# Four large scalings of an output pass, each with its store, cut in two halves

## The chip, the cores and the metric

The kernel runs on one core of one Trainium2 chip. The metric is the device time of one execution in microseconds (us), as the median of several runs. A profiled execution of the same program supplies the trace.

## The reference

The input `x` has 384 x 384 positions of 384 channels, in bfloat16 (one batch). The kernel scales every channel by a gate worked out from that channel's mean over all positions:

```python
g = jnp.einsum("bhwc->bc", x) / (H * W)
s = jax.nn.sigmoid(g * w1d[0])        # k = 1
return x * s[:, None, None, :]
```

So the whole input has to be summed before the first output can be written: 113 MB are read, the gate is found, and 113 MB are written. The on-chip memory does not hold the whole input.

## The kernel before, in words

**Rows.** The 147456 positions are spread over 128 partitions, 1152 rows of 384 channels to each partition. A "row" below is one such row on all 128 partitions, 96 KB. The chip's memory holds an `arena` of 275 rows. A load or a store of n rows is one DMA of 128 pieces of n x 768 bytes. The chunk `STREAMED` (784 rows and one more) passes through the arena and is read a second time later; the chunk `KEPT` stays on the chip between the passes.

**Pass one** loads all rows and sums them on TensorE into the PSUM tile `acc`. Part of the kept rows is packed meanwhile: in a group, the fourth row of every four is hidden in unused bits of the other three (`fold`), so that three rows of memory hold four. There are ten groups (`GROUPS`), of 16, 24 or 32 rows; the last is kept in PSUM banks (`BANKED`). Then ScalarE works out the gate (`s_bf`, with a copy `s_ps` in PSUM).

**Pass two** follows an order that is written out by hand, `PLAN2`. Its entries, with arena addresses:
- `("M", a, n, m)`: scale n rows from address a. DVE (VectorE) does the first n - m rows and POOL (GpSimd) the last m; POOL's part first waits for the DVE instruction that stands before DVE's part (`scale_both`).
- `("W", a, n)`: store n rows from address a (`store`).
- `("L", a, n)`: load the next n streamed rows to address a (`load`).
- `("U", g, a, m)`: the next of five steps that unpack group g: `fields`, `signs` and `three` are bit operations on DVE (lines 280 and 286), `threefold` and `fourth` scale its rows.
- `("B", a)`: bring the PSUM group back to the arena (ScalarE).

Scaling is line 444, storing line 465, loading line 240.

**Order and waits.** Every engine goes through its own entries in the order written. All loads and stores are issued by SP (SyncE) on one queue, in the order of the `W` and `L` entries. The class `Flow` keeps for every row who wrote it and who read it, and puts a semaphore wait in front of an instruction for each such dependence: a store waits for the scalings of its own rows, a load waits for the stores that still read the rows it overwrites. An SP instruction that waits holds up all SP instructions behind it. The semaphores of SP's DMAs go round in 24 lanes, and a DMA also waits for the one 24 before it.

Of the kernel before, what the change touches and what calls it, by code (L numbers as in the profile page):

```python
# [131 lines left out]
def kernel(  # L132
# [13 lines left out]
    B, H, W, C = x.shape  # L146
# [14 lines left out]
    U = 3 * PIECE + PAIRS * 3 * PAIR  # L161
# [424 lines left out]
    for a, n in ((U, 4), (U + 4, 4), (V, 4)):  # L586
# [102 lines left out]
```

## Time and profile before

| | |
|---|---|
| median of 3 runs | 722.63 us (722.34 to 723.5) |
| profiled execution | 719.44 us, of which the trace's span is 717.3 us |
| data moved | 303.70 MB, mean 423 GB/s over the span |
| busy time: DVE, POOL, ACT, PE | 468.8, 119.1, 116.5, 223.3 us |
| chain that ended last | DMA 44%, DVE 29%, PE 16% of the span |

The trace's times count from its first instruction. Pass one ends at about 268 us; pass two takes the rest. In the page's slices each digit is the busy share of one fortieth of the span, in tenths. The chain of work follows back from the last instruction, at each step to what released it. For a DMA the trace has the time of its issue on SP and the time from issue to landing (all its bytes at their place).

### The profile page before, as it was taken

Reading aid. Unit: us, or ns where it says so; the run is one execution under the profiler, and the core shown is the slowest. Engines: PE = TensorE matmul, PEld = TensorE weight load, DVE = VectorE, ACT = ScalarE, POOL = GpSimd, SP = SyncE. Lnnn points to the kernel's source line nnn. Section 1 sums busy time; section 2 is a strip of 40 time slices with the busy share of each in tenths; the row PEclk is TensorE's granted clock in tenths of the full one; section 3 lists DMA queues with packets and bytes.
Section 4 is the critical chain, followed back from the end, with each engine's and each line's share of the span. In section 5 each row is a group of like instructions: output and inputs, shape, how many; then the busy total and the mean of one; then the engine's idle time right before and its main releaser. Section 6 shows DMA issues by size and latency. Waiting matters only on the chain.

```text
span 717.3 us, 2076 instructions
## 1 busy us (share of the span) xinstructions
PE 223.3 (31%) x1279; PEld 0.3 (0%) x3; DVE 468.8 (65%) x359; ACT 116.5 (16%) x97; POOL 119.1 (17%) x43
## 2 busy tenths in 40 slices
PE   4577977999998880000000000000000000000000
PEld 0000000000000000000000000000000000000000
DVE  4600001798989849997999999979189950366800
ACT  3700001576767630000000020000000000000000
POOL 0000000000000006608024143562114400000000
PEclk9889988999999995555555555555555555555555
DMA  9999999999999989999999999999999999999997
GB/s 378 429 445 422 434 441 437 430 433 426 427 426 428 431 334 386 399 428 432 432 430 438 432 434 433 450 413 451 415 456 426 434 437 401 455 439 396 450 426 323
DMA packets 15853, 303.70 MB, mean 423 GB/s; under 512 B 1762, under 2 KB 2402, under 8 KB 5474
## 3 DMA queue, kind: packets, MB, share of 16 engines
q1 hardware_dynamic: 15840, 303.57, 98.9%
q8 instruction: 5, 0.08, 0.0%
q14 instruction: 6, 0.05, 0.0%
q10 hardware_dynamic: 2, 0.00, 0.0%
HBM read 190.32 MB, written 113.25 MB: 423 GB/s over the span
## 4 chain that ended last, share of the span: by engine, by line
DMA 44%; DVE 29%; PE 16%; POOL 2%; DVEq 1%; ACT 1%; issue 1%; SPq 0%; POOLq 0%
DMA arena<-in_x_dram 33%; DVE arena L444 17%; PE bank L246 16%; DMA out_dram<-arena 11%; DVE arena L280 7%; DVE arena L286 5%; POOL arena L444 2%; DVEq L107 1%; ACT arena L317 1%; SPq L240 0%; ACT s_bf L431 0%; SPq L465 0%; SPq L113 0%; POOLq L113 0%; SPq L684 0%
## 5 line engine op out<-in xcount | busy, mean ns | idle before, releaser
L280 DVE TENSOR_SCALAR arena<-arena 128x1536 uint16<-128x1536 uint16 (+2 forms) x199 | 149.4, 795 | 128.3 <-DMA arena<-in_x_dram 98.5
L246 PE MATMUL bank<-arena,ones 128*128 128x384 bf16 x1151 | 202.8, 339 | 35.4 <-DMA arena<-in_x_dram 35.3
L444 POOL TENSOR_TENSOR arena<-arena,s_bf 128x1536 bf16<-128x1536 bf16 (+7 forms) x39 | 118.9, 3062 | 444.7 <-ACT bank L435 268.2
L444 DVE TENSOR_TENSOR arena<-arena,bank 128x1152 bf16<-128x1152 bf16 (+21 forms) x57 | 159.9, 2846 | 7.4 <-DMA arena<-in_x_dram 7.0
L317 ACT ACTIVATE arena<-arena 128x3072 uint16<-128x3072 uint16 (+1 forms) x38 | 102.5, 2696 | 146.0 <-DVE arena L280 146.0
L286 DVE TENSOR_TENSOR arena<-arena 128x3072 uint16<-128x3072 uint16 (+2 forms) x90 | 117.6, 1307 | 13.0 <-PE bank L246 10.1
L541 PE MATMUL bank<-odd,ones 128*128 128x1 bf16 x1 | 0.2, 187 | 316.2 <-DVE odd L536 316.2
L444 DVE TENSOR_TENSOR arena<-arena,s_bf 128x11136 bf16<-128x11136 bf16 (+4 forms) x7 | 46.6, 6699 | 59.0 <-DMA arena<-in_x_dram 48.6
L382 ACT COPY arena<-bank 128x512 uint32<-128x512 uint32 (+2 forms) x8 | 4.2, 534 | 155.3 <-DMA out_dram<-arena 155.1
L246 PE MATMUL bank<-s_bf,ones 128*128 128x384 bf16 x125 | 22.1, 326 | 0.0
L317 ACT ACTIVATION_READ_ACCUMULATOR arena<-arena 128x1 f32 x38 | 7.1, 187 | 0.0
L382 ACT COPY bank<-arena 128x512 uint32<-128x512 uint32 (+2 forms) x8 | 3.8, 527 | 0.0
L260 PE MATMUL bank<-arena,ones 128*128 128x384 bf16 x1 | 0.5, 478 | 6.6 <-DMA arena<-in_x_dram 6.6
L431 ACT ACTIVATE s_bf<-bank,w_sc 128x384 bf16<-128x384 f32 x1 | 0.6, 581 | 9.7 <-PE bank L246 9.7
L657 ACT ACT_TABLE_LOAD x1 | 1.3, 1283 | 0.7 <-PEq L673 0.7
L347 DVE TENSOR_SCALAR w_sc<-bank 128x1 f32<-128x1 f32 x1 | 0.2, 160 | 1.3 <-PE bank L342 1.3
L342 PE MATMUL bank<-w_bf,ones 1*128 1x1 bf16 x1 | 0.2, 182 | 2.5 <-DMA w_bf<-in_w1d_dram 2.5
L337 DVE MEMSET ones<- 128x128 bf16 x1 | 0.2, 165 | 1.0 <-PEq L673 1.0
L541 PEld LDWEIGHTS bank<-odd,ones 128*128 128x128 bf16 x1 | 0.1, 105 | 574.4 <-DVE odd L536 574.4
L545 DVE CAST odd_i<-bank 128x1 int32<-128x1 f32 x1 | 0.2, 157 | 0.3 <-PE bank L541 0.3
L435 ACT COPY bank<-s_bf 128x192 uint32<-128x192 uint32 x1 | 0.3, 323 | 0.0
L382 ACT COPY arena<-rest 128x64 uint32<-128x64 uint32 x1 | 0.2, 245 | 0.0
(10 smaller groups left out, 1.4 us busy)
## 6 DMA issues: line engine op xcount, KB each, us to landing
arena<-in_x_dram SPq DMA_DIRECT2D x4, 8160.0 KB, 39.5
out_dram<-arena SPq DMA_DIRECT2D x4, 8160.0 KB, 26.7
out_dram<-arena SPq DMA_DIRECT2D x7, 3072.0 KB, 23.7
arena<-in_x_dram SPq DMA_DIRECT2D x6, 3072.0 KB, 19.4
arena<-in_x_dram SPq DMA_DIRECT2D x3, 4608.0 KB, 24.5
arena<-in_x_dram SPq DMA_DIRECT2D x2, 4992.0 KB, 23.3
arena<-in_x_dram SPq DMA_DIRECT2D x2, 4512.0 KB, 36.9
out_dram<-arena SPq DMA_DIRECT2D x2, 4512.0 KB, 26.2
```

The costliest lines, as they stand in the source:

```text
L107: with self.tc.tile_critical(sync_engine=mybir.EngineType.Pool, no_gpsimd_drain=True):
L246: return pe.add_instruction(mybir.InstMatmult(name=nc.get_next_instruction_name(), ins=[pe.lower_ap(rhs), pe.lower_ap(ones[:])], outs=[pe. ...
L260: return nc.tensor.matmul(acc, lhsT=ones[:], rhs=arena[:, i, :], start=first, stop=last)
L280: lambda: nc.vector.tensor_scalar(out=dst, in0=src, scalar1=s0, scalar2=s1, op0=op0, op1=op1),
L286: "DVE", lambda: nc.vector.tensor_tensor(out=dst, in0=a, in1=b, op=op), reads=reads, writes=writes
L317: lambda: nc.scalar.activation(out=y, in_=y, func=ACTF.Copy, accum_out=seen[:, 2 * k + i : 2 * k + i + 1]),
L382: "ACT", lambda: nc.scalar.copy(dst.bitcast(u32), src.bitcast(u32)), reads=reads, writes=writes
L431: lambda: nc.scalar.activation(out=s_bf[:], in_=acc, func=ACTF.Sigmoid, scale=w_sc[:, 0:1]),
L435: "ACT", lambda: nc.scalar.copy(s_ps.bitcast(u32), s_bf[:].bitcast(u32)), reads=["s_bf"], writes=["bank0"]
L444: lambda: vec.tensor_tensor(out=v, in0=v, in1=s[:, None, :].to_broadcast([P, n, C]), op=Op.mult),
L541: lambda: nc.tensor.matmul(votes, lhsT=ones[:], rhs=odd[:], start=True, stop=True),
L657: nc.scalar.preload_act_table(ACTF.Sigmoid)
```

## The change

Four `M` entries of `PLAN2` become two each, and so do the `W` entries that store their rows:
- 47 rows at 220 become 24 and 23; POOL's part of 6 becomes 3 and 3. The store of the first half stands ahead of, that of the second half behind, group 8's `threefold` step.
- 54 rows at 44 become 27 and 27; POOL's part of 6 becomes 3 and 3.
- 85 rows at 172 become 43 and 42; POOL's part of 17 becomes 8 and 9.
- 85 rows at 20 (the second of three times that this address holds 85 rows) become 43 and 42, all on DVE.

The order of the other entries on each engine stays. SP has four more stores. Nothing else is changed.

```diff
-        ("M", 220, 47, 6), ("U", 8, 188, 0), ("W", 220, 47), ("M", 98, 10, 5), ("U", 8, 188, 2), ("U", 1, 12, 0),
+        ("M", 220, 24, 3), ("M", 244, 23, 3), ("W", 220, 24), ("U", 8, 188, 0), ("W", 244, 23), ("M", 98, 10, 5), ("U", 8, 188, 2), ("U", 1, 12, 0),
...
-        ("U", 1, 12, 5), ("W", 12, 32), ("M", 44, 54, 6), ("U", 6, 164, 0), ("W", 44, 54), ("B", 196), ("L", 221, 46),
+        ("U", 1, 12, 5), ("W", 12, 32), ("M", 44, 27, 3), ("M", 71, 27, 3), ("W", 44, 27), ("U", 6, 164, 0), ("W", 71, 27), ("B", 196), ("L", 221, 46),
...
-        ("M", 172, 85, 17), ("M", 20, 85, 0), ("W", 172, 85), ("U", 0, 0, 0), ("W", 20, 85), ("W", 0, 16),
+        ("M", 172, 43, 8), ("M", 215, 42, 9), ("W", 172, 43), ("M", 20, 43, 0),
+        ("W", 215, 42), ("M", 63, 42, 0), ("W", 20, 43), ("U", 0, 0, 0), ("W", 63, 42), ("W", 0, 16),
```

## The prediction

> **What bounds the kernel now.** I read the page's slices first, then its chain, then SP's waits, then stage sums of pass two, and last the single DMAs around the four edits. The page, first for the span, the sixteen DMA engines and the chain:
>
> ```profile
> span 717.3 us, 2076 instructions
> DMA  9999999999999989999999999999999999999997
> GB/s 378 429 445 422 434 441 437 430 433 426 427 426 428 431 334 386 399 428 432 432 430 438 432 434 433 450 413 451 415 456 426 434 437 401 455 439 396 450 426 323
> DMA 44%; DVE 29%; PE 16%; POOL 2%; DVEq 1%; ACT 1%; issue 1%; SPq 0%; POOLq 0%
> ```
>
> Pass two fills the slices from the fifteenth on. From the seventeenth to the last but one the DMA engines stand at 9 tenths or more. The chain nevertheless gives DVE 29% of the span, and SP's own waits between 376 and 590 us, where all four edits lie, are mostly for DVE's scalings (line 444):
>
> ```profile
> SPq L113 <- DVE arena L444: 148.7, 12, 24.5
> SPq L465 <- DVE arena L444: 16.7, 1, 16.7
> ```
>
> Read alone, these rows say that stores come late because scalings are long. What matters is whether the DMA engines run out of work while SP waits. Stage sums (last two columns: share of time in which the DMA engines are busy, GB/s; packets count where they start, so a stage's rate wobbles at its edges):
>
> ```profile
> 376.00:443.00 67.00, 0.00 (x0) 0.00 (x0) 64.88 (x29) 4.41 (x9) 24.30 (x8) 0.50 1.01 435
> 443.00:542.00 99.00, 0.00 (x0) 0.00 (x0) 76.17 (x51) 0.00 (x0) 35.39 (x13) 0.50 1.00 434
> 542.00:608.00 66.00, 0.19 (x1) 0.10 (x1) 41.70 (x16) 0.00 (x0) 14.26 (x3) 0.50 0.99 428
> 608.00:714.00 106.00, 0.00 (x0) 0.00 (x0) 46.28 (x6) 0.00 (x0) 0.00 (x0) 0.50 0.99 427
> ```
>
> They do not: 0.99 to 1.01 in every stage. The chain's pieces with their lengths, and single issues (SP's timeline: start, length; the DMA view of the same instant: KB, us from issue to landing), show how:
>
> ```profile
> 416.37 9.77 DVE arena L444
> 426.20 16.93 DMA out_dram<-arena
> 549.04 33.00 DVE arena L444 x3
> 582.06 25.57 DMA out_dram<-arena
> 607.64 44.66 DMA arena<-in_x_dram
> ```
>
> ```profile
> 373.39 0.34 SPq L465 DMA_DIRECT2D out_dram<-arena  x1
> out_dram<-arena SPq DMA_DIRECT2D x1, 2880.0 KB, 17.4
> 385.78 0.33 SPq L465 DMA_DIRECT2D out_dram<-arena  x1
> out_dram<-arena SPq DMA_DIRECT2D x1, 4512.0 KB, 15.7
> 417.83 0.33 SPq L465 DMA_DIRECT2D out_dram<-arena  x1
> out_dram<-arena SPq DMA_DIRECT2D x1, 3072.0 KB, 13.1
> 542.75 0.34 SPq L465 DMA_DIRECT2D out_dram<-arena  x1
> out_dram<-arena SPq DMA_DIRECT2D x1, 3072.0 KB, 26.4
> 565.04 0.34 SPq L465 DMA_DIRECT2D out_dram<-arena  x1
> out_dram<-arena SPq DMA_DIRECT2D x1, 8160.0 KB, 23.4
> 583.52 0.33 SPq L465 DMA_DIRECT2D out_dram<-arena  x1
> out_dram<-arena SPq DMA_DIRECT2D x1, 1536.0 KB, 27.8
> 679.12 0.33 SPq L465 DMA_DIRECT2D out_dram<-arena  x1
> out_dram<-arena SPq DMA_DIRECT2D x1, 4512.0 KB, 36.8
> ```
>
> SP's DMAs land in the order of issue, each one its own bytes behind the one before. The first 85-row store lands at 565.04 + 23.4 = 588.4, the second at 582.06 + 25.57 = 607.63, 19.2 us later; 19.2 / 85 = 0.226 us a row (96 KB). The 85-row load issued at 607.64 lands at 652.30; ahead of it stand 16, 29 and 67 rows, and (16 + 29 + 67 + 85) x 0.2263 = 44.58 us of the 44.67 between the two landings. So the finish is a queue's: bytes over rate, as long as the queue is never empty. Its stock at the four stores now split is what was still to land when each was issued:
> - 47 rows at 220: 373.39 + 17.4 = 390.8, less 385.78: 5.0 us.
> - 54 rows at 44: 417.83 + 13.1 = 430.9, less 426.20: 4.7 us.
> - 85 rows at 172: 542.75 + 26.4 = 569.15, less 565.04: 4.1 us.
> - 85 rows at 20: 588.4 - 582.06: 6.3 us.
>
> What must be in stock is an empty queue's start-up. Nearest row, a store of one row near the start of pass two:
>
> ```profile
> 268.64 0.35 SPq L465 DMA_DIRECT2D out_dram<-arena  x1
> out_dram<-arena SPq DMA_DIRECT2D x1, 96.0 KB, 1.6
> ```
>
> 1.6 us, of which 0.2 is its bytes: some 1.4 us. The thinnest stock, 4.1, is above that by 2.7.
>
> **The change part by part.** Durations of the scalings, by form (count, total us, mean ns of one):
>
> ```profile
> L444 DVE TENSOR_TENSOR arena<-arena,bank 128x32640 bf16<-128x32640 bf16 x1 | 17.1, 17145 | 0.0
> L444 DVE TENSOR_TENSOR arena<-arena,bank 128x26112 bf16<-128x26112 bf16 x1 | 13.7, 13746 | 0.0
> L444 DVE TENSOR_TENSOR arena<-arena,bank 128x15744 bf16<-128x15744 bf16 x1 | 8.3, 8341 | 0.0
> L444 DVE TENSOR_TENSOR arena<-arena,bank 128x9216 bf16<-128x9216 bf16 x5 | 24.6, 4947 | 4.3 <-DMA arena<-in_x_dram 4.3
> L444 DVE TENSOR_TENSOR arena<-arena,bank 128x1536 bf16<-128x1536 bf16 x8 | 7.6, 951 | 0.2
> L444 POOL TENSOR_TENSOR arena<-arena,s_bf 128x6528 bf16<-128x6528 bf16 x1 | 12.6, 12625 | 1.4 <-DVE arena L444 1.4
> L444 POOL TENSOR_TENSOR arena<-arena,s_bf 128x1536 bf16<-128x1536 bf16 x15 | 46.4, 3096 | 342.6 <-ACT bank L435 268.2 <-DVE arena L286 39.9 <-DVE arena L280 27.1
> ```
>
> DVE: between 4 rows (951 ns) and 85 rows (17145 ns) lie 81 rows, 0.200 us each, so an instruction costs 0.15 us beside its rows. POOL: (12625 - 3096) / 13 = 0.733 us a row and 0.16 beside.
>
> 1. **Four more DVE scalings.** 41 rows become 21 + 20 (4.35 + 4.15 for 8.34), 48 become 24 + 24 (2 x 4.95 for the chain's 9.77), 68 become 35 + 33 (7.15 + 6.75 for 13.75), 85 become 43 + 42 (8.75 + 8.55 for 17.15): 0.15 us more each, 0.6 in all, on DVE. Behind them in DVE's order stand the threefold scaling of group 8, the unfolding of group 6, the second 85-row block and the fourth step of group 0; their stores move 0.15 to 0.3 us, and the stock above covers that. Cost on the path: 0. With no stock it would be 0.6 us.
>
> 2. **Three more POOL scalings** (6 rows become 3 + 3 twice, 17 become 8 + 9; the block at 20 gives POOL none). POOL's second half waits for DVE's first half, a wait that is new. At 172: POOL's 8 rows take 6.0 us beside DVE's 7.15, its 9 rows 6.8 beside 6.75, so both end within 0.2 us of each other. At 44 and 220, 3 rows (2.4 us) stand beside 4 to 5 us of DVE. No store gets later than by 0.2. Cost: 0.
>
> 3. **Four more stores, each first half issued earlier.** Issue now, less the whole scaling, plus its first half: 220 at 385.78 - 8.34 + 4.35 = 381.8, 44 at 426.20 - 9.77 + 4.95 = 421.4, 172 at 565.04 - 13.75 + 7.15 = 558.4, 20 at 582.06 - 17.15 + 8.75 and 0.15 for the split before it = 573.8; the second halves 0.15 us later than the whole now (0.3 at 20): 385.9, 426.4, 565.2 and 582.4. The stock at these eight issues, all bytes in order at 0.2263 us a row: 9.0 and 10.3, 9.5 and 10.6, 10.7 and 13.7, 14.6 and 15.7 us. No byte is saved, and every later DMA lands behind the same rows as before. Price of a store as such, in a full queue: the 44.67 us above hold four DMAs and exceed their rows by 0.09, so 0.02 us each. Upper end: an empty queue's 1.4 us, 5.6 in all. Below nothing: the most that a fuller queue could give back. From the landing of the 47 rows at 401.5 (385.78 + 15.7) to the last at 715.9 (679.12 + 36.8) the order written out moves 1377 rows (its stores and loads from the 10 rows at 98 on), 1377 x 0.2263 = 311.6 of 314.4 us; so 2.8 us, if every hiccup of the transfers vanished. I take 4 x 0.02 = 0.1 us, from the row nearest in kind (large DMAs behind others).
>
> The Trainium skill ("DMA: Bandwidth & Descriptors", Anatomy of one DMA) fits about 2.0 us plus bytes over 436 GB/s for one DMA, on GpSimd's path, most of it the receipt of the last write. Charged one after another, that would make the four stores cost 8 us; the trace's 0.02 us says that behind other transfers it overlaps. The rate agrees: 96 KB in 0.2263 us is 434 GB/s.
>
> 4. **Waits and later loads.** SP waits for two events where it waited for one. Behind the second half at 20 stand the 16-row store and the loads of 29, 67, 85 and 47 rows; these come 0.15 to 0.3 us later, with 15.7 us in stock. The 67-row load overwrites rows of the first half at 172 alone, which now lands at 569.15 + 43 x 0.2263 = 578.9, not 588.4; it follows the 29-row load at about 585. The 85-row load still needs both halves at 20, the same 85 rows ahead of it: 607.7. The last 85-row and 47-row scalings are not split, so the tail keeps its shape.
>
> Sum: 0.1 us on the profiled execution's 719.44 us (717.3 span and 2.1 around it). The median of the runs, 722.63, stands 3.2 above that execution; put on it: 722.7.
>
> **The rivals.** About 0.2%, 1.4 us, is what a measurement of this kernel can tell from no change.
>
> *A, faster: the chain is right.* If the first half's early start freed buffers earlier, the 85-row load at 607.64 would come once a 42-row store issued at 582.4 lands on its own: 582.4 + 9.5 + 1.4 = 593.3, 14.3 us earlier: 708.4. The Trainium skill says so for one condition ("Perfetto Trace Analysis", DMA Optimizations): smaller DMAs may end sooner where the DMA engines are generally idle. Against A: both halves queue behind the store from 565.04 on, and the engines are at 0.99 in that stage. Chance 2%. A small version: undisturbed runs, 3.2 us longer than the profiled one, may run short of stock at 4.1 us where the profile does not; then the deeper stock gives back at most the 2.8 us: 719.8. Chance 5%.
>
> *B, slower: every store pays its start-up, even in a full queue.* 4 x 1.4 = 5.6 us: 728.2. It decides from 0.36 us a store on. For it: one row took 1.6 us. Against: 0.02 us a DMA between 607.6 and 652.3. Chance 5%.
>
> *C, slower: a half waits for POOL and the queue runs dry.* Place: the second half at 172, whose POOL rows begin only when DVE's first half is done. Should POOL's 9 rows start after DVE's second half instead, they would end 6.8 us late, at 572; the stock then is 578.9 - 572 = 7 us, still above 1.4. It decides only if POOL is more than 13.7 - 1.4 = 12.3 us late; at 14 the queue idles for 1.7 us: 724.4. Chance 2%.
>
> *D, no change that can be measured:* the forecast, 86%; the split then only deepens a stock that was enough.
>
> **How the numbers follow.** 722.7 is D's. D's own range is the runs' spread about it, 722.0 to 723.7. For eight in ten and a little more I go down by 1.8, two thirds of the 2.8 us of A's small version (720.9), and up by 0.4 us a store, just past where B decides (724.3). Faster by over 0.2%: A's 7%, less the small version's part below 1.4 us: 0.06. Slower: B and C, 0.07. Same: 0.87.
>
> **What would show it.** In the changed profile: the DMA share 0.99 to 1.01 in all stages; first halves issued 4 to 8 us earlier; the second 42-row store landing near 607.7 and the next 85-row load near 652.4; the 67-row load issued near 585; four added DVE rows, 0.15 us each. The prediction is wrong if the spacing of landings exceeds their rows by over 0.3 us at the split stores (B), if a stage's DMA share falls (C), or if the landing at 607.6 moves by over 1 us (A).

## The result

The changed kernel took 718.71 us in the median of 4 runs (717.02 to 719.37), the kernel before 723.07 us (722.34 to 723.75): a ratio of 0.9936 (of the means, as all ratios below), 95% interval 0.9915 to 0.9957. Two later sets gave 0.9959 (0.9944 to 0.9973) and 0.9964 (0.9948 to 0.9979). In time that is 4.6, 3.0 and 2.6 us. The first set flatters the change: the kernel before has 723.07 us there, in 4 runs, but medians of 720.8 to 721.6 in five later sets of 22 to 35, while the changed kernel stays at 718.4 to 718.7. So the change makes the kernel some 3 us faster, clear of the 0.2% that can be told. I had forecast no change.

The profiled execution of the changed kernel hardly shows it: 719.37 us with a span of 717.1 us, beside 719.44 and 717.3 before. The page's lines, the waits of SP's queue between 376 and 590 us, and the stage sums:

```profile
span 717.1 us, 2093 instructions
DMA  9999999999999989999999999999999999999997
GB/s 376 431 446 418 438 430 424 451 415 434 431 427 429 427 344 381 399 429 431 432 430 429 446 418 442 432 434 447 410 450 448 407 437 421 448 436 419 455 423 312
```

```profile
SPq L113 <- DVE arena L444: 148.6, 15, 24.6
SPq L465 <- DVE arena L444: 16.3, 2, 8.1
```

```profile
376.00:443.00 67.00, 0.00 (x0) 0.00 (x0) 63.95 (x30) 4.41 (x9) 24.16 (x9) 0.50 1.01 434
443.00:542.00 99.00, 0.00 (x0) 0.00 (x0) 76.18 (x52) 0.00 (x0) 34.71 (x13) 0.50 1.00 434
542.00:608.00 66.00, 0.19 (x1) 0.10 (x1) 42.97 (x18) 0.00 (x0) 15.58 (x4) 0.50 0.99 428
608.00:714.00 106.00, 0.00 (x0) 0.00 (x0) 46.28 (x6) 0.00 (x0) 0.00 (x0) 0.50 0.99 428
```

SP waits as long for DVE as before (148.7 and 16.7 us then), only in more pieces, and the DMA share is the same to the hundredth in all four stages. None of these views of the two executions can tell the kernels apart. The single transfers can. The chain's pieces, then issues on SP's timeline (start, length), then the DMA view of two of these issues (KB, us to landing), the 32-row store at 543.89 and the load at 609.24:

```profile
550.19 33.13 DVE arena L444 x5
583.34 25.52 DMA out_dram<-arena
608.87 44.53 DMA arena<-in_x_dram
```

```profile
381.88 0.33 SPq L465 DMA_DIRECT2D out_dram<-arena  x1
422.53 0.33 SPq L465 DMA_DIRECT2D out_dram<-arena  x1
543.89 0.34 SPq L465 DMA_DIRECT2D out_dram<-arena  x1
559.59 0.34 SPq L465 DMA_DIRECT2D out_dram<-arena  x1
574.87 0.33 SPq L465 DMA_DIRECT2D out_dram<-arena  x1
609.24 0.43 SPq L240 DMA_DIRECT2D arena<-in_x_dram  x1
```

```profile
out_dram<-arena SPq DMA_DIRECT2D x1, 3072.0 KB, 26.3
...
arena<-in_x_dram SPq DMA_DIRECT2D x1, 4512.0 KB, 54.8
```

The first halves are issued 3.7 to 7.2 us earlier, as forecast: at 381.88 for 381.8, and at 422.53, 559.59 and 574.87, each some 1.1 us behind the forecast; this execution was late by that much already where the 54-row load landed (417.48 for 416.35). The stock at 172 is 543.89 + 26.3 - 559.59 = 10.6 us instead of 4.1. The last row of the second and of the third fence is the 47-row load near the end. It lands at 609.24 + 54.8 = 664.0, and the 85-row load ahead of it at 653.40: 10.6 us for 47 rows, just its bytes (47 x 0.2263 = 10.64). In the kernel before:

```profile
608.01 0.68 SPq L240 DMA_DIRECT2D arena<-in_x_dram  x1
```

```profile
arena<-in_x_dram SPq DMA_DIRECT2D x1, 4512.0 KB, 56.2
```

608.01 + 56.2 = 664.2, behind a landing at 652.30: 11.9 us. This load lost 1.3 us, in the only execution of the kernel before that I had, and I had counted that among the "hiccups".

### The profile page after: what moved, and what is told of

The parts are those of the page before. It is cut to its first block, busy times and chain, and to the rows that moved or that the text cites. A ratio compares the mean times of both kernels' runs of the same rounds, so it can differ in the third digit from the quotient of the medians.

```text
span 717.1 us, 2093 instructions
## 1 busy us (share of the span) xinstructions
PE 220.9 (31%) x1279; PEld 0.3 (0%) x3; DVE 469.3 (65%) x363; ACT 116.5 (16%) x97; POOL 119.6 (17%) x46
## 4 chain that ended last, share of the span: by engine, by line
DMA 47%; DVE 31%; PE 11%; ACT 2%; POOL 1%; DVEq 1%; issue 1%; SPq 0%; POOLq 0%
DMA arena<-in_x_dram 37%; DVE arena L444 20%; PE bank L246 11%; DMA out_dram<-arena 10%; DVE arena L280 7%; DVE arena L286 4%; ACT arena L317 2%; POOL arena L444 1%; DVEq L107 1%; SPq L465 0%; SPq L240 0%; ACT s_bf L431 0%; SPq L113 0%; DVEq L113 0%; SPq L685 0%
## 5 line engine op out<-in xcount | busy, mean ns | idle before, releaser
L246 PE MATMUL bank<-arena,ones 128*128 128x384 bf16 x1151 | 200.4, 337 | 38.0 <-DMA arena<-in_x_dram 37.9
L444 POOL TENSOR_TENSOR arena<-arena,s_bf 128x1536 bf16<-128x1536 bf16 (+6 forms) x42 | 119.4, 2854 | 446.5 <-ACT bank L435 268.5
L444 DVE TENSOR_TENSOR arena<-arena,bank 128x1152 bf16<-128x1152 bf16 (+22 forms) x61 | 160.1, 2669 | 8.1 <-DMA arena<-in_x_dram 7.6
L260 PE MATMUL bank<-arena,ones 128*128 128x384 bf16 x1 | 0.5, 479 | 7.0 <-DMA arena<-in_x_dram 7.0
```

The costliest lines, as they stand in the source:

```text
L246: return pe.add_instruction(mybir.InstMatmult(name=nc.get_next_instruction_name(), ins=[pe.lower_ap(rhs), pe.lower_ap(ones[:])], outs=[pe. ...
L260: return nc.tensor.matmul(acc, lhsT=ones[:], rhs=arena[:, i, :], start=first, stop=last)
L444: lambda: vec.tensor_tensor(out=v, in0=v, in1=s[:, None, :].to_broadcast([P, n, C]), op=Op.mult),
```

## The experiments

**The two kernels again, and the change in two parts.** The first four runs shared one chip.

```diff
e1_after   the whole change        e2_before  nothing changed
e3_85s     ("M",172,43,8) ("M",215,42,9) ("W",172,43) ("M",20,43,0) ("W",215,42) ("M",63,42,0) ...; 220 and 44 whole
e4_47_54   ("M",220,24,3) ("M",244,23,3) ... ("M",44,27,3) ("M",71,27,3) ...; 172 and 20 whole
```

> The changed kernel again, beside runs of the kernel before on the same chip. Theory Q (in most executions, unlike the profiled one, the kernel before lets its DMA queue run dry where the stock was thinnest): ratio 0.993 to 0.995, 3.6 to 5 us faster. Theory N (the two sets of runs were taken on occasions that differ by some us, and the programs are equal, as their profiled executions of 719.4 us are): ratio 0.999 to 1.001.

> The kernel before, unchanged, as if it were a new one. Both theories expect a ratio of 1.000 within 0.001; a ratio farther off would show how much two sets of runs of one program differ, and would speak for N. Its runs' spread shows whether executions of 719.4 us and of 722.6 us both occur in this program (Q needs that).

> Only the two 85-row blocks are halved (stock before 4.1 and 6.3 us). Q: the thinnest stock is here, so most of the gain, ratio 0.994 to 0.997. N: 0.999 to 1.001.

> Only the 47-row and the 54-row block are halved (stock before 5.0 and 4.7 us). Q: the rest of the gain, ratio 0.996 to 1.000. N: 0.999 to 1.001.

Measured: the changed kernel 0.9959 (0.9944 to 0.9973); the kernel before as a new one 0.9999 (0.9985 to 1.0012); the two 85-row blocks 0.9963 (0.9947 to 0.9978); the two smaller 0.9985 (0.9973 to 0.9998). So theory N falls, and what Q expects of `e3_85s` and `e4_47_54` came; the whole change gained a little less than Q's 0.993 to 0.995. The twelve executions of the kernel before run from 718.38 to 722.35 us, those of the changed kernel from 717.80 to 719.25. The traced execution on which my prediction rested, 719.44 us, was one of the quick ones.

A trace of a longer one (`e2_before`, 721.22 us) shows more. Its issues of the 32-row store, of the 85-row store at 172 behind it and of the last 47-row load, and from the DMA view KB and us to landing of the first and the last of them:

```profile
544.92 0.34 SPq L465 DMA_DIRECT2D out_dram<-arena  x1
567.21 0.34 SPq L465 DMA_DIRECT2D out_dram<-arena  x1
609.75 0.81 SPq L240 DMA_DIRECT2D arena<-in_x_dram  x1
```

```profile
out_dram<-arena SPq DMA_DIRECT2D x1, 3072.0 KB, 25.9
...
arena<-in_x_dram SPq DMA_DIRECT2D x1, 4512.0 KB, 56.3
```

```profile
609.38 44.61 DMA arena<-in_x_dram
```

The stock at 172 is 544.92 + 25.9 - 567.21 = 3.6 us here. The last fence is the chain's piece for the 85-row load, which lands at 653.99; the 47-row load lands at 609.75 + 56.3 = 666.05, 12.06 us behind it: 1.4 us lost.

A landing is the arrival of a DMA's last part. The trace has sixteen completions of each DMA. The Trainium skill ("DMA: Bandwidth & Descriptors", Why a DMA increments its semaphore by 16 and not by 1) says that these come from the DMA engines, which finish independently; the traces agree, with 1.1 to 3.6 us between the first and the last completion of the 30-row store near 391 us. Below, that distance is called the lead, and the engine that completes first the foremost. In this trace the foremost engine finishes the 32-row store 3.49 us before the last one. For it the stock at 172 is 3.65 - 3.49 = 0.16 us: it runs dry, and by the next landing its lead has shrunk to 2.43 us. It is not alone: thirteen of the sixteen had under 1.4 us left, and twelve fell back by 0.3 us or more, 10 us in sum. That gave theory S.

**Stores or scalings, one block, and no halves at all.** All on a second chip.

```diff
e5_stores    ("M",172,85,17) ("M",20,85,0) whole; ("W",172,43) ("W",215,42) ... ("W",20,43) ("W",63,42)
e6_scalings  ("M",172,43,8) ("M",215,42,9) ("M",20,43,0) ("M",63,42,0); ("W",172,85) ... ("W",20,85) whole
e7_172       ("M",172,43,8) ("M",215,42,9) ("W",172,43) ("M",20,85,0) ("W",215,42) ...
e8_early172
-  ("U",2,116,4), ("U",0,0,0), ("U",0,0,0), ("W",116,32), ("U",0,0,0), ("U",0,0,1), ("M",172,85,17),
+  ("U",2,116,4), ("M",172,85,17), ("U",0,0,0), ("U",0,0,0), ("W",116,32), ("U",0,0,0), ("U",0,0,1),
```

> At the two 85-row blocks only the stores are halved; the scalings stay whole, so that both halves of a store are issued when the whole scaling is done. Theory S (stock: of the 16 DMA engines the ones that are ahead run dry at the store issued near 565 us, since its stock of some 4 us is hardly more than their lead of 2.5 to 3.6 us; they fall back into step with the others, and the 47-row load near 660 us then loses some 1.4 us): as before, ratio 0.999 to 1.001, and the load's stall stays. Theory P (size of the stores' pieces, 33 KB instead of 65 KB a partition, is what helps): 0.995 to 0.997, the stall gone.

> At the two 85-row blocks only the scalings are halved; each store stays whole behind its second half. S and P both expect what was before: ratio 0.999 to 1.001, the 47-row load's stall of some 1.4 us there. A gain here would speak for something in DVE or POOL (theory V).

> Only the 85 rows at 172 are halved, scaling and store; the block at 20 stays whole. S: the thin stock is at 172, so all the gain of both: ratio 0.995 to 0.997, no fall of the engines' lead at the landing near 590 us, no stall in the 47-row load. P: half the gain, 0.997 to 0.999.

> Nothing is halved: the whole scaling of 85 rows at 172 stands ahead of the four steps of group 0's unpacking on DVE instead of behind them, so that its store is issued near 556 us instead of 565 (stock 13 us instead of 4). The number and the sizes of all DMAs, and their order, are those of before. S: 0.995 to 0.997, the stall gone. P: 0.999 to 1.001.

Measured: stores alone 0.9996 (0.9980 to 1.0012); scalings alone 1.0013 (0.9998 to 1.0028); the 172 block 0.9994 (0.9977 to 1.0010); the early scaling 0.9985 (0.9971 to 1.0000). Neither smaller stores (P) nor shorter scalings (V) help by themselves; a whole scaling that merely stands earlier seems to. S had expected more of the last two, 0.995 to 0.997, so it had the price too high. In the traces the stall goes exactly as S has it: the 47-row load loses 1.47 and 1.49 us with the halved stores and the halved scalings, and 0.08 and 0.00 with the 172 block halved and with the early scaling. Of `e8_early172`, the chain's piece for the 85-row load, SP's issue of the 47-row load, and its KB and us to landing:

```profile
608.73 44.57 DMA arena<-in_x_dram
```

```profile
609.10 0.73 SPq L240 DMA_DIRECT2D arena<-in_x_dram  x1
```

```profile
arena<-in_x_dram SPq DMA_DIRECT2D x1, 4512.0 KB, 54.8
```

It lands at 663.9, 10.6 us behind 653.29, although all DMAs have the order and the sizes of before. DVE runs the same scalings during this load in `e2_before` and in `e8_early172`, so they are not what differs. The time of `e7_172` is no proof: its interval holds both S's 1.4 us and nothing.

**The block at 20, both cures together, and repeats.** On a third chip.

```diff
e9_20            ("M",172,85,17) ("M",20,43,0) ("W",172,85) ("M",63,42,0) ("W",20,43) ("U",0,0,0) ("W",63,42)
e10_early172_20  as e8_early172, and ("M",20,43,0) ("W",172,85) ("M",63,42,0) ("W",20,43) ("U",0,0,0) ("W",63,42)
e11_172_again    as e7_172         e12_early172_again  as e8_early172
```

> Only the 85 rows at 20 are halved; the block at 172 stays whole and its store comes near 565 us with a stock of 4 us. Theory S (the thin stock at 172 is the cause, and it costs the 47-row load near 660 us its 1.4 us): the stall is there, ratio 0.999 to 1.001. Theory T (both thin stocks, at 172 and at 20, cost something, and in executions that no trace has shown the second does too): 0.997 to 0.999.

> The whole scaling at 172 stands early on DVE (as in the run that halved nothing), and the block at 20 is halved. S: as with the early scaling alone, 0.997 to 0.999, no stall in the 47-row load. T: all that the change brings, 0.995 to 0.997, from one split instead of four.

> The kernel with only the 172 block halved again, for its time (0.9994 before, with an interval of 0.0016 to either side) and a second trace. S: 0.997 to 0.999 and no stall at the 47-row load in the trace. T: the same time; a stall at that load, if the execution is a long one.

> The kernel with the early whole scaling at 172 again, for its time (0.9985 before, interval 0.9971 to 1.0000) and a second trace. S and T: 0.997 to 0.999; S: no stall at the 47-row load.

Measured: only 20 halved 1.0002 (0.9988 to 1.0017), stall 1.82 us; early scaling and 20 halved 0.9989 (0.9975 to 1.0003), 0.06 us; the 172 block again 0.9993 (0.9979 to 1.0007), 0.01 us; the early scaling again 0.9977 (0.9962 to 0.9993), 0.01 us. The time of the early scaling is now clear of no change, and that of the 172 block alone is not, in either set, though its stall is gone in both traces. The halves at 20 bring nothing that shows, alone or on top; T falls as far as it rests on them.

**What the rest of the gain is.** Run together on one chip.

```diff
e13_after_again  as e1_after       e14_85s_again  as e3_85s       e16_before_again  as e2_before
e15_early172_47_54  as e8_early172, and the halves at 220 and 44 as in e4_47_54
```

> The changed kernel again on one chip with the next three. Theory S (only the stall after the thin stock at 172 is saved, 1.2 to 1.9 us): ratio 0.9973 to 0.9985. Theory T (something else of 1 us or more is saved besides): 0.994 to 0.997. Both: no stall at the 47-row load in the trace.

> Only the two 85-row blocks halved, again. S: 0.9973 to 0.9985. T, if the second saving lies at the halves at 20: 0.994 to 0.997. Both: no stall at the 47-row load.

> The early whole scaling at 172, with the 47-row and the 54-row block halved as in the change; the block at 20 whole. S: 0.9973 to 0.9985. T, if the second saving lies at the smaller halves: 0.994 to 0.997.

> The kernel before again, as a further trace and as the measure of what two sets of one program differ by: 0.9988 to 1.0012. S and T: the stall of 1.2 to 1.9 us at the 47-row load is in the trace, and the lead of the fastest DMA engine falls at the landing near 590 us if it was over 2.7 us before.

Measured: the changed kernel 0.9964 (0.9948 to 0.9979); the two 85-row blocks 0.9982 (0.9966 to 0.9998), so the first 0.9963 was probably a lucky set; early scaling with the smaller halves 0.9967 (0.9951 to 0.9983); the kernel before 1.0003 (0.9988 to 1.0018), with a stall of 1.47 us. So the second saving lies at the smaller halves, and it adds up: 0.9985 for them alone, 0.9977 to 0.9985 for the early scaling alone, 0.9967 together.

In the traces all of it fits one rule, found after the fact. The table, worked out from the completions of each DMA in the traces (`before` and `after` are the two first traces of all, `e17_by_2us` and `e18_after_early` are told of below), has the stock of the foremost engine when a store is issued (previous DMA's first completion less the issue, us), and the time that a certain later load took beyond its bytes (us):

```
                      store at 220 -> 54-row load | at 44 -> next 85-row load | at 172 -> last 47-row load
before                   3.54   0.37              |  2.88   0.20              |  1.63   1.32
e2_before                2.49   0.63              |  1.81   1.39              |  0.16   1.45
e16_before_again         2.58   0.43              |  1.91   1.53              |  0.12   1.47
e5_stores                2.00   1.16              |  1.10   1.63              |  0.06   1.47
e6_scalings              0.98   1.47              |  1.49   1.52              |  0.04   1.49
e9_20                    2.53   0.86              |  1.71   1.71              |  0.04   1.82
e4_47_54                 5.33  -0.04              |  6.27   1.15              |  0.03   1.43
e17_by_2us               1.68   1.58              |  1.35   1.50              |  2.45   0.02
e3_85s                   2.52   0.22              |  2.00   1.45              |  6.66   0.03
e14_85s_again            3.60   0.19              |  3.28   0.05              |  8.80   0.00
e7_172                   3.54   0.24              |  3.33   0.14              |  8.76   0.08
e11_172_again            3.19   0.35              |  2.42   0.73              |  7.25   0.01
e8_early172              2.52   0.03              |  2.15   0.98              |  9.48   0.00
e12_early172_again       1.33   1.48              |  1.49   1.16              |  9.52  -0.01
e10_early172_20          2.59   0.97              |  1.67   1.13              |  9.70   0.06
after                    7.54   0.75              |  6.71   0.14              |  7.42   0.04
e1_after                 7.00   0.45              |  7.18   0.05              |  7.93   0.02
e13_after_again          7.24  -0.02              |  7.83   0.61              |  7.99   0.01
e15_early172_47_54       7.72   0.14              |  8.25   0.35              | 11.11   0.26
e18_after_early          7.14   0.21              |  7.30   0.47              | 16.61   0.00
```

At 172, seven traces with a stock of at most 1.63 us have a stall of 1.32 to 1.82, thirteen with 2.45 and more have 0.26 at most. At 44, the nine with at most 2.00 have 1.13 to 1.71; of the other eleven ten have 0.05 to 0.98, and `e4_47_54` has 1.15: there the 32-row store just ahead of the halves had only 1.73 us. At 220 the four with at most 2.00 have 1.16 to 1.58, the others at most 0.97. So a loss of over 1.1 us comes, but for that one, where the foremost engine's stock is at most some 2 us. The line is not sharp: 0.7 to 1.0 us are lost at 2.15 to 2.6 us in some rows, and 0.75 once at 7.54. Two pairs speak for the stock and against the lead as such: `e17_by_2us` and `e2_before` come to the 172 store with leads of 3.47 and 3.49 us, and `e4_47_54` and `e12_early172_again` to the 30-row store near 391 us with 3.3 us each; in both pairs only the one with the thin stock (0.16 and 1.33 us) has the loss beside it in the table.

**How much stock is enough, and whether more helps.** One kernel moves the whole scaling ahead of one step of group 0 only, the other moves the changed kernel's halves ahead of all four.

```diff
e17_by_2us       -  ("U",0,0,0), ("U",0,0,1), ("M",172,85,17), ("M",20,85,0)
                 +  ("U",0,0,0), ("M",172,85,17), ("U",0,0,1), ("M",20,85,0)
e18_after_early  +  ("U",2,116,4), ("M",172,43,8), ("M",215,42,9), ("U",0,0,0), ("U",0,0,0), ("W",116,32), ...
```

> The kernel before with the whole scaling of 85 rows at 172 moved ahead of the one threefold step of group 0 (2.3 us on DVE); no halves. Its store comes near 562.7 us with a stock of some 6.5 us. Theory S with the criterion stock less lead of the fastest engine (up to 3.6 us) over 1.4 us: no fall of the lead at that store's landing, no stall at the 47-row load, ratio 0.9973 to 0.9990. If a deep stock is needed: the stall stays, 0.999 to 1.001.

> The changed kernel with its two halves at 172 also moved ahead of group 0's first step, so that their stores come near 550 and 557 us. S: the stock there was already enough, so the time of the changed kernel, ratio 0.995 to 0.9975 against the kernel before. If more stock always helps: below 0.995.

Measured: 0.9994 (0.9978 to 1.0010) and 0.9966 (0.9950 to 0.9982). In the trace of `e17_by_2us` the stock at 172 is 5.92 us, 2.45 for the foremost engine; its lead stays at 3.47, and the 47-row load loses 0.02 us, as S's criterion has it; the time's interval holds both S's gain and none. The criterion fails in `before`, the trace on which the prediction rested: with 1.63 us, over 1.4, no engine fell back there (the lead is 2.49 us before the 172 store and 2.48 at its landing), and yet the load lost 1.32 us. A thin stock goes with the stall, then, even where no engine runs dry. More stock at 172 does not help beyond the change. No version beat the changed kernel by more than its interval.

## Why the prediction was wrong

Right, step by step: the halves cost DVE and POOL what was worked out. Forms of the changed kernel:

```profile
L444 DVE TENSOR_TENSOR arena<-arena,bank 128x16512 bf16<-128x16512 bf16 x1 | 8.7, 8746 | 0.0
L444 DVE TENSOR_TENSOR arena<-arena,bank 128x16128 bf16<-128x16128 bf16 x1 | 8.5, 8545 | 0.0
L444 DVE TENSOR_TENSOR arena<-arena,bank 128x13440 bf16<-128x13440 bf16 x1 | 7.1, 7146 | 0.0
L444 POOL TENSOR_TENSOR arena<-arena,s_bf 128x3456 bf16<-128x3456 bf16 x1 | 6.8, 6765 | 1.0 <-DVE arena L444 1.0
```

8.75, 8.55, 7.15 and 6.8 us were forecast. The eight stores of halves take 0.02 to 0.04 us each beyond their rows, but for one at 0.13 and one at 0.27. The second 42-row store landed at 608.85 and the next 85-row load at 653.40, both about 1 us behind the forecast, so the landing at 607.6 moved by over 1 us, but the wrong way for A; between the two lie 44.5 us where there were 44.67, so the large A did not come. `e5_stores` speaks against B too: two more stores, 2.8 us by B, and 0.9996. C did not occur: the second half at 172 was issued at 566.38, 6.8 us behind the first, as POOL's 6.77 us allow.

Wrong are two steps.

First, "What must be in stock". I took the queue for one queue and its stock from landings, 4.1 us against a start-up of 1.4, "above that by 2.7". There are sixteen engines, each with its own share of every DMA, and a landing is the last one's. The foremost was 2.5 us ahead in the execution that I read (1.63 us of stock, hardly over 1.4) and 3.4 to 3.6 us in the six other traces with the late 172 store (0.03 to 0.16); in those six, twelve to fourteen engines fell back there. Of the 2.7 us that I called cover 0.2 was left. The DMA share of 0.99 could not show it, as no engine ran dry in that execution; even where so many did, the stage from 542 to 608 us has 0.97 to 0.99. With this cover, part 3 put what a fuller queue gives back at nothing.

Second, the bound "2.8 us, if every hiccup of the transfers vanished". It was taken from one execution, one of the quick ones, and read as noise of the transfers. 1.3 us of it was a stall that returned at the same load in each of the seven traces with a thin stock. In most longer executions one or two more such stalls come, at the 54-row load and at the first 85-row load. `e5_stores` loses 1.16 + 1.63 + 1.47 = 4.3 us in the three together, the changed kernel in its second trace 0.5.

The nearest case of mine was the small version of A, at 5% and 719.8: executions that run short of stock where the profiled one does not. The sign and the place were right, and the two later sets (3.0 and 2.6 us) came near its price. That is luck: the 2.8 us were all the losses of one quick execution, while the gain comes from stalls that are mostly in the longer ones. Wrong was the chance: such executions were the rule and not the exception.

What is shown: the stall at the last 47-row load depends on when the 172 store is issued and not on halves, sizes or number of DMAs, and its 1.3 to 1.8 us are near the 1.1 us (0.9985) that the eight runs with only that cured gain on average (0.9963, 0.9982, 0.9994, 0.9993, 0.9985, 0.9977, 0.9989, 0.9994). The smaller halves are worth about as much (0.9985 alone; 0.9959 to 0.9967 in the four later sets with both cured). That they too work by the earlier issue is argued from the table: no run issued those stores earlier without halving them. Not shown is why a load loses over a microsecond after an engine has come close to running dry, and why at these three loads, of which only the first comes soon behind its store. The foremost engine's own idling can't be it, since the last engine sets the end. The traces do show what the stall looks like: of the 128 pieces of the 47-row load, which take 1.34 us each, 13 to 22 take 1.6 to 3.1 us in the seven stalled traces, all begun within some 4 us between 659 and 665 us; in the other thirteen at most 2 do, with 1.64 at most. So it looks as if many engines are held up at about the same moment; by what, the traces do not tell. A stall also occurs without a late store ahead of it: a 60-row load in pass one, landing near 68.5 us, loses 1.03 to 1.53 us in all twenty traces.

## What to carry to other kernels

A queue of transfers that is 99% busy can still be fed too late: take each store's or load's stock from the first of the sixteen completions, not from the landing. Here losses came where it fell under some 2 us, a little above the start-up of 1.4. The cure is to issue earlier; at 172 a scaling moved ahead of work that nobody waits for did as well as one cut in two. Before a bound is taken from one execution's stalls, look whether the same transfer stalls in a second trace, and where the profiled execution lies among the timed ones.

## What the runs showed of the hardware

The sixteen DMA engines drift apart, and the drift differs from execution to execution: at the landing of the 30-row store near 391 us the foremost was between 1.1 and 3.6 us ahead, with the same program up to there. What varies most is not the foremost engine but the last: the first completion of that store comes between 388.7 and 389.5 us in the twenty traces, the last between 390.0 and 392.8. Each stall widened the lead (in `e2_before` from 2.64 to 3.49 us over the 85-row load that lost 1.39), which thins the foremost engine's stock at the next store: one stall so prepares the next. The traces with a lead of 1.1 us near 391 had no stall over 0.4 us from there on. This fits the spread of the times, 3 to 6 us for the kernel before and 1.0 to 2.4 for the changed one (718.00 to 718.99 in the set of twelve), but it is not the whole of it: the 2.8 us by which the 30-row store's landing varies are there ahead of every edit. The shortest executions of the two kernels hardly differ (717.94 and 717.02 us); what the change takes away are the long ones.
